# Key cache in 8 MB loads of 64 KB runs through three half-shared slots, value chunks in pairs behind them

## The chip, the cores and the metric

The kernel runs on one core of a Trainium2 chip. The metric is the device time of one execution in microseconds (us), taken as the median of several runs. The profile is one further execution, taken by the hardware profiler; its times count from the start of its span. TensorE is called PE there, VectorE DVE, ScalarE ACT, GpSimd POOL and SyncE SP.

## The reference

One decode step of a layer, for a batch of two, in float32:

```python
xn = layernorm(x)                                    # x: [2, 1, 512]
q = (xn @ wq) -> [2, 32 heads, 1, 128]
scores = q . k / sqrt(128)                           # k_cache: [2, 8, 32768, 128], 4 query heads share a key head
o = softmax(scores) . v                              # v_cache: the same shape
s = o -> [2, 1, 4096] @ wo
g = silu(relu(xn @ w1 + b1) ** 2 @ w2 + b2)
return x + s * g
```

Keys and values are 268.4 MB each, and each is read once; the weights are 24.1 MB together. The arithmetic on each byte is small.

## The kernel before, in words

A **stream** is one pair of batch and key head: there are 16 (`NS`), and a stream has 32768 keys and as many values of 128 numbers. A stream is cut into four **chunks** of 8192 keys, 4 MB each (`CHUNK`, 32 KB in each of the 128 partitions), so there are 64 chunks of keys and 64 of values (`NK`). Each is one DMA from SP's queue: `load_k` (L91) takes from each partition's 256 keys (128 KB in a row in memory) the quarter `u`, a run of 32 KB; `load_v` (L98) takes 4 MB in a row, 32 KB of it for each partition.

All big loads go through one ring of `BUFS` = 4 buffers of 32 KB (L55). The order of the loads is written out in the list `loads` (L126 to L136): the two halves of `wq`, then keys and values in turn, values four chunks behind the keys, `w1` and `w2` early on, `wo` last. A load is issued when `free` says that a buffer is there; `give()` frees one after the last instruction that reads it. So three loads are queued or on their way while one buffer is worked on.

The work on a chunk `n`:

- `scores(n)` (L237): eight DVE transposes (L246) of 128x1024 numbers turn the keys into `kt` tiles (a pool of 8 buffers); after each four of them PE multiplies the queries `qz` with them into the PSUM bank `sc[t]` (L251). Then `give()`, and a DVE maximum over the bank (`rm`, L255).
- `softmax(s)` (L257) after the fourth chunk: a short chain over DVE and PE finds the maximum (L259 to L268), four ACT exponentials (L272) fill `p`.
- `probs(s)` (L280): 16 PE transposes of `p` (L286) with four ACT copies to `pT` (L287), and a small product `l_ps` (L292) for the sum.
- `values(n)` (L302): 16 PE products of `pT` with the value chunk into `o_ps` (L309); the profile counts each as two instructions. After a stream's fourth chunk the result is scaled and turned into `oT` and `oW` (L316 to L329).

`mlp_up` and `mlp_down` (L334, L350) compute the gate early on. At the end `project` (L387) multiplies `oW` with `wo`, whose last quarter comes in four pieces, and L399 to L402 write the result.

The order of instructions on an engine isn't quite that of the text: the framework goes through the program with durations of its own, and an instruction whose inputs are there may be placed ahead of one that is written earlier and still waits. What each engine then executes is in that fixed order.

Of the kernel before, what the change touches and what calls it, by code (L numbers as in the profile page):

```python
# [9 lines left out]
F32 = mybir.dt.float32  # L10
# [4 lines left out]
P = 128  # L15
# [4 lines left out]

NG = 4
RUN = 64
CHUNK = P * RUN
NO = 16
BUFS = 4
NEG = -3.0e38
PIECES = ((0, 4), (4, 6), (6, 7), (7, 8))

# [2 lines left out]
def gqa_decode_kernel(ctx: ExitStack, tc: tile.TileContext, x, kc, vc, wq, wo, w1, b1, w2, b2, out):  # L33
    nc = tc.nc
    B, _, D = x.shape
# [4 lines left out]
    ND = D // P  # L40
# [11 lines left out]
    out2 = out.rearrange("b s d -> (b s) d")  # L52

    const = ctx.enter_context(tc.tile_pool(name="const", bufs=1))
    ring = ctx.enter_context(tc.tile_pool(name="ring", bufs=BUFS))  # L55
    ktpool = ctx.enter_context(tc.tile_pool(name="ktpool", bufs=8))
    work = ctx.enter_context(tc.tile_pool(name="work", bufs=2))
    pms = ctx.enter_context(tc.tile_pool(name="pms", bufs=2, space=bass.MemoryType.PSUM))
# [3 lines left out]
        return pms.tile([P, 512], F32, tag="ms", name=name)  # L62


    xt = const.tile([P, D], F32, name="xt")
    b1t = const.tile([NG, FG], F32, name="b1t")
    b2t = const.tile([1, D], F32, name="b2t")
    nc.vector.memset(xt, 0.0)
    nc.scalar.dma_start(xt[:B, :], x2)
    nc.scalar.dma_start(b1t, b1.rearrange("(g f) -> g f", g=NG))  # L70
# [8 lines left out]
    def rows(cache, s):  # L79
        hkv, b = divmod(s, B)  # L80
        return cache[b, hkv]

    def load_wq(i):
        t = ring.tile([P, 2, wq.shape[1]], F32, tag="r", name=f"wq{i}")
        nc.sync.dma_start(t, wq.rearrange("(p d) f -> p d f", p=P)[:, 2 * i:2 * i + 2, :])
        return t

    def load_k(m):
        s, u = divmod(m, NCH)
        t = ring.tile([P, RUN, DH], F32, tag="r", name=f"k{m}")  # L90
        nc.sync.dma_start(t, rows(kc, s).rearrange("(p t r) d -> p t r d", p=P, t=NCH)[:, u])  # L91
        return t

    def load_v(m):
        s, u = divmod(m, NCH)
        t = ring.tile([P, RUN, DH], F32, tag="r", name=f"v{m}")
        src = rows(vc, s)[u * CHUNK:(u + 1) * CHUNK].rearrange("(p r) d -> p r d", p=P)
        nc.sync.dma_start(t, src)  # L98
        return t

    def load_w1(_):
        t = ring.tile([P, ND, F], F32, tag="r", name="w1")
        nc.sync.dma_start(t, w1.rearrange("(p d) f -> p d f", p=P))
        return t

    def load_w2(_):
        t = ring.tile([P, FJ, D], F32, tag="r", name="w2")
        nc.sync.dma_start(t, w2.rearrange("(p j) e -> p j e", p=P))
        return t


    def load_wo(i):
        if i % 2 == 0:
            wide[i // 2] = ring.tile([P, 2, WG, D], F32, tag="r", name=f"wo{i // 2}")
        t = wide[i // 2][:, i % 2]
        src = wo[i * WG * P:(i + 1) * WG * P, :].rearrange("(p j) e -> p j e", p=P)
        if i < NWG - 1:
            nc.sync.dma_start(t, src)
        else:
            for j0, j1 in PIECES:  # L120
                nc.sync.dma_start(t[:, j0:j1, :], src[:, j0:j1, :])
        return t

    wide = {}
    NK = NS * NCH
    loads = [(1, load_wq, 0), (1, load_wq, 1)]  # L126
    for m in range(NK + NCH):
        if m < NK:
            loads.append((1, load_k, m))
        if m == 1:  # L130
            loads.append((1, load_w1, 0))
        if m == 2:
            loads.append((1, load_w2, 0))
        if m >= NCH:
            loads.append((1, load_v, m - NCH))
    loads += [(1 - i % 2, load_wo, i) for i in range(NWG)]  # L136
    free = [BUFS]
    done = [0]

    def issue():  # L140
        while done[0] < len(loads) and free[0] >= loads[done[0]][0]:
            bufs, f, a = loads[done[0]]
            free[0] -= bufs
            tiles[f, a] = f(a)
            done[0] += 1

    def take(f, a):
        return tiles.pop((f, a))

    def give():  # L150
        free[0] += 1
        issue()

    issue()
# [37 lines left out]
    nc.scalar.activation(st[:, 2:3], st[:, 1:2], AF.Sqrt)  # L192
    nc.vector.reciprocal(st[:, 3:4], st[:, 2:3])
    nc.vector.tensor_scalar(xn, xn, st[:, 3:4], None, op0=ALU.mult)  # L194
    xnT = const.tile([P, ND, P], F32, name="xnT")
# [3 lines left out]
    nc.vector.tensor_copy(xnT.rearrange("p a b -> p (a b)"), t_ps)  # L199


    for i in range(2):
        wqt = take(load_wq, i)
        for d2 in range(2):
            d = 2 * i + d2
            for f in range(2):
                for g in range(NG):
                    cc = f * NG + g
                    nc.tensor.matmul(sc[f][32 * g:32 * g + 32, :], xnT[:, d, 0:32],  # L209
                                     wqt[:, d2, cc * 512:(cc + 1) * 512], start=(d == 0), stop=(d == ND - 1))  # L210
        give()
    qT = const.tile([P, B, HKV, REP, 4], F32, name="qT")
    for f in range(2):
        for h in range(REP):
# [20 lines left out]
    rm, pr, pT, rs = {}, {}, {}, {}  # L235

    def scores(n):  # L237
        s, t = divmod(n, NCH)
        if t == 0:
            rm[s] = work.tile([P, NCH], F32, tag="rm4", name=f"rm4_{s}")  # L240
        kt = take(load_k, n)
        for e0 in range(0, 4, 2):
            kts = []
            for g in range(NG):
                r = ktpool.tile([P, 2, NO, 32], F32, tag="kt", name=f"kt{n}_{e0}_{g}")
                nc.vector.transpose(r.rearrange("p e o w -> p o e w"),  # L246
                                    kt[:, g * NO:(g + 1) * NO, e0 * 32:(e0 + 2) * 32].rearrange("p o (e w) -> p o e w", e=2))
                kts.append(r)
            for e in range(2):
                for g in range(NG):  # L250
                    nc.tensor.matmul(sc[t][32 * g:32 * g + 4 * REP, :], qz[s % 2][:, e0 + e, :],  # L251
                                     kts[g][:, e].rearrange("p o w -> p (o w)"),
                                     start=(e0 + e == 0), stop=(e0 + e == 3))
        give()
        nc.vector.tensor_reduce(rm[s][:, t:t + 1], sc[t], axis=AX.X, op=ALU.max)  # L255

    def softmax(s):  # L257
# [21 lines left out]

    def probs(s):  # L280
        p, lh = pr.pop(s)
        sb = work.tile([P, NG, 4, NO, REP], F32, tag="pT", name=f"pT{s}")
        for i in range(NO // 4):
            t_ps = misc(f"pT_ps{s}_{i}")
            for j in range(4):
                nc.tensor.transpose(t_ps[:, j * P:(j + 1) * P], p[:, 4 * i + j].rearrange("p w t -> p (w t)"), ident)  # L286
# [15 lines left out]
    def values(n):  # L302
# [3 lines left out]
        for i in range(NO // 4):  # L306
            for g in range(NG):
# [1 line left out]
                nc.tensor.matmul(o[32 * g:32 * g + 16, :], pT[s][:, g, a, 4 * i:4 * i + 4, :].rearrange("p o h -> p (o h)"),  # L309
                                 vt[:, lo:lo + 4, :].rearrange("p o d -> p (o d)"),  # L310
                                 start=(a == 0 and i == 0), stop=(a == NCH - 1 and i == NO // 4 - 1))
        give()
        if a == NCH - 1:
            hkv, b = divmod(s, B)
            o_sb = work.tile([P, 512], F32, tag="o_sb", bufs=1, name=f"o_sb{s}")
# [5 lines left out]
            nc.vector.tensor_copy(oT[:, hkv * REP:(hkv + 1) * REP, b], t_ps[:, :REP])  # L321
            if hkv % 2 == 1:
                i = hkv // 2
                m = work.tile([P, WG, P // WG], F32, tag="om", name=f"om{s}")
# [4 lines left out]
                nc.scalar.copy(oW[:, i, :, b], t_ps[:, :WG])  # L329


    hT, gate = const.tile([P, FJ, 32], F32, name="hT"), const.tile([P, DE], F32, name="gate")

    def mlp_up():  # L334
        wt = take(load_w1, 0)
# [6 lines left out]
        give()  # L342
# [7 lines left out]
    def mlp_down():  # L350
# [9 lines left out]
        give()  # L360
        e = work.tile([P, DE], F32, tag="e", name="e")
        nc.scalar.activation(e, y_ps[:, :DE], AF.Sigmoid)
        nc.vector.tensor_mul(gate, e, y_ps[:, :DE])


    for n in range(NK + NCH):
        s, t = divmod(n, NCH)
        if n < NK:
            if t == 0:
                set_q(s)  # L370
            scores(n)
        if n == 1:
            mlp_up()
        if n == 2:
            mlp_down()
        if s >= 1 and t == 0:
            probs(s - 1)
        if n < NK and t == NCH - 1:
            softmax(s)
        if n >= NCH:  # L380
            values(n - NCH)


    a_ps = sc[0]
# [9 lines left out]
        project(i, 0, WG)  # L394
    for j0, j1 in PIECES:
        project(NWG - 1, j0, j1)
    asb = work.tile([P, DE], F32, tag="e", name="a_sb")
# [28 lines left out]
```

## Time and profile before

| | |
|---|---|
| median of 3 runs | 1316.15 us (1316.07 to 1316.32) |
| profiled execution, its own time | 1315.98 us |
| its span, first to last instruction | 1314.2 us |
| bytes read from HBM | 561.01 MB, 427 GB/s over the span |
| PE busy / DVE busy / ACT busy | 946.4 us (72%) / 675.2 us (51%) / 107.5 us (8%) |
| mean granted TensorE clock | 0.861 |
| keys: DMAs, size, median from issue to landing | 64 of 4096 KB, 29.6 us |
| values: the same | 64 of 4096 KB, 29.6 us |

The profile's page lists busy times of the engines, a strip of 40 slices of the span with the busy share in tenths, the DMA queues, the chain of work that ended last, the costliest groups of instructions, and the DMA issues. Beside it the trace can be asked for the instructions in order of time (the timeline), for who waited for whom (the waits), for the chain in order of time, and for the busy time of each engine in chosen windows. It also holds a record of every DMA packet: its start, size and duration, and for each DMA the 16 completion marks of the 16 DMA engines. "Landing" is the moment at which the last of these is there.

### The profile page before, as it was taken

To read this page: it belongs to the slowest core of one execution; us is meant where nothing else is said; L and a number is where in the kernel's file an instruction comes from. 1 tells how busy PE (TensorE), PEld (TensorE's weight loads), DVE (VectorE), ACT (ScalarE), POOL (GpSimd) and SP (SyncE) were. 2 spreads that over 40 slices of the span, in tenths; PEclk is the share of its full clock that TensorE was granted. 3 is DMA by queue.
4 is the path that set the end of the run, shared out by engine and by line. 5 is a ranking of instruction groups with operands and counts; after the bars stand their busy time and mean duration, and the time that the engine had idled before them with its cause. 6 is when DMAs were issued, how large, how long until landed. Compare 5 with 4: busy or idle time off the path is not lost.

```text
span 1314.2 us, 11662 instructions
## 1 busy us (share of the span) xinstructions
PE 946.4 (72%) x5054; PEld 245.7 (19%) x5054; DVE 675.2 (51%) x778; ACT 107.5 (8%) x237; POOL 15.1 (1%) x76
## 2 busy tenths in 40 slices
PE   4777786876868677776776778586686767668666
PEld 1121121212112121111212112121211212112123
DVE  4765564553655465465454556355365546446510
ACT  0010000101001010100101001010100101010010
POOL 1000000000000000000000000000000000000000
PEclk9989888988888878887887988898887887888798
DMA  9999999999999999999999999999999999999997
GB/s 412 425 436 430 431 430 430 429 431 431 431 432 431 430 430 430 431 431 430 431 431 430 430 431 430 431 434 430 432 431 432 429 433 432 430 430 432 430 431 310
DMA packets 20113, 561.76 MB, mean 427 GB/s; under 512 B 2247, under 2 KB 2267, under 8 KB 2654
## 3 DMA queue, kind: packets, MB, share of 16 engines
q1 hardware_dynamic: 20024, 561.00, 99.3%
q8 instruction: 39, 0.64, 0.2%
q14 instruction: 12, 0.10, 0.0%
q10 hardware_dynamic: 38, 0.02, 0.0%
HBM read 561.01 MB, written 0.00 MB: 427 GB/s over the span
## 4 chain that ended last, share of the span: by engine, by line
DMA 76%; DVE 22%; PE 1%; issue 0%; ACTq 0%; DVEq 0%
DMA k<-in_A_k_cache 71%; DVE kt L246 22%; DMA v<-in_A_v_cache 2%; DMA wo<-in_A_wo 2%; PE sc L209 1%; DMA xt<-in_A_x 1%; PE y_ps L358 0%; PE sc L251 0%; PE xnT_ps L198 0%; DVE sq L189 0%; DVE xnT L199 0%; DVE st L190 0%; DVE st L186 0%; DVEq L246 0%; ACTq L70 0%
## 5 line engine op out<-in xcount | busy, mean ns | idle before, releaser
L251 PE MATMUL sc<-kt,qz 128*16 128x512 f32 x2048 | 605.6, 695 | 276.9 <-DVE kt L246 256.2
L246 DVE STREAM_TRANSPOSE kt<-k 128x1024 f32<-128x1024 f32 x512 | 584.3, 1207 | 288.3 <-DMA k<-in_A_k_cache 288.3
L309 PE MATMUL o_ps<-v,pT 128*16 128x512 f32 x2048 | 272.9, 604 | 11.5 <-DMA v<-in_A_v_cache 11.5
L251 PEld LDWEIGHTS sc<-kt,qz 128*16 128x16 f32 x2048 | 94.1, 100 | 768.9 <-DVE kt L246 652.0
L272 ACT ACTIVATE p<-sc,nm 128x512 f32<-128x512 f32 x64 | 68.8, 1198 | 1025.4 <-DVE nm L268 1025.4
L255 DVE TENSOR_REDUCE rm<-sc 128x1 f32<-128x512 f32 x64 | 44.3, 692 | 126.3 <-PE sc L251 126.3
L309 PEld LDWEIGHTS o_ps<-v,pT 128*16 128x16 f32 x2048 | 66.1, 98 | 169.9 <-issue 152.0
L286 PE MATMUL pT_ps<-ident,p 128*128 128x128 f32 x256 | 52.1, 381 | 0.1
L286 PEld LDWEIGHTS pT_ps<-ident,p 128*128 128x128 f32 x256 | 46.3, 205 | 5.6 <-issue 2.6
L320 PE MATMUL oT_ps<-rs,o_sb 128*128 128x4 f32 x128 | 19.2, 273 | 34.3 <-ACT o_sb L316 34.3
L275 DVE TENSOR_REDUCE l<-l 128x1 f32<-128x4 f32 x16 | 2.5, 154 | 66.9 <-ACT p L272 66.9
L294 DVE RECIPROCAL r<-l_ps 128x4 f32<-128x4 f32 x16 | 2.9, 183 | 56.5 <-PE l_ps L292 56.5
L321 DVE COPY oT<-oT_ps 128x4 f32<-128x4 f32 x16 | 2.6, 163 | 51.7 <-PE oT_ps L320 51.7
L287 ACT COPY pT<-pT_ps 128x256 f32<-128x256 f32 x64 | 23.9, 373 | 45.7 <-PE pT_ps L286 45.1
L320 PEld LDWEIGHTS oT_ps<-rs,o_sb 128*128 128x128 f32 x128 | 17.8, 215 | 48.3 <-ACT o_sb L316 48.3
L232 POOL COPY qz<-qT 32x16 f32<-32x16 f32 x64 | 12.8, 200 | 1081.4 <-PE sc L251 1051.2
L261 PE MATMUL mx_ps<-ident,rm 128*128 128x128 f32 x16 | 5.1, 319 | 15.8 <-DVE rm L259 15.8
L272 ACT ACTIVATION_READ_ACCUMULATOR p<-sc,nm 128x1 f32 x64 | 14.6, 228 | 0.0
L316 ACT COPY o_sb<-o_ps 128x512 f32<-128x512 f32 x16 | 9.7, 604 | 31.0 <-PE o_ps L309 31.0
L198 PE MATMUL xnT_ps<-ident,xn 128*128 128x128 f32 x4 | 1.1, 428 | 15.2 <-DVE xn L194 15.2
L390 PE MATMUL sc<-wo,oW 128*32 128x128 f32 x256 | 8.8, 275 | 3.4 <-DMA wo<-in_A_wo 3.3
L209 PE MATMUL sc<-wq,xnT 128*32 128x512 f32 x64 | 10.0, 792 | 0.8 <-DVE xnT L199 0.8
(67 smaller groups left out, 107.5 us busy)
## 6 DMA issues: line engine op xcount, KB each, us to landing
k<-in_A_k_cache SPq DMA_DIRECT2D x64, 4096.0 KB, 29.6
v<-in_A_v_cache SPq DMA_DIRECT2D x64, 4096.0 KB, 29.6
wq<-in_A_wq SPq DMA_DIRECT2D x2, 4096.0 KB, 12.2
w<-in_B_w SPq DMA_DIRECT2D x2, 3584.0 KB
wo<-in_A_wo SPq DMA_DIRECT2D x3, 2048.0 KB
wo<-in_A_wo SPq DMA_DIRECT2D x1, 1024.0 KB
wo<-in_A_wo SPq DMA_DIRECT2D x1, 512.0 KB
wo<-in_A_wo SPq DMA_DIRECT2D x2, 256.0 KB, 29.4
```

Source lines behind the costliest of these rows:

```text
L209: nc.tensor.matmul(sc[f][32 * g:32 * g + 32, :], xnT[:, d, 0:32], wqt[:, d2, cc * 512:(cc + 1) * 512], start=(d == 0), stop=(d == ND - 1))
L232: nc.gpsimd.tensor_copy(qz[s % 2][32 * a:32 * a + 32, :, a * REP:(a + 1) * REP], qT[32 * a:32 * a + 32, b, hkv].rearrange("p h e -> p e h"))
L246: nc.vector.transpose(r.rearrange("p e o w -> p o e w"), kt[:, g * NO:(g + 1) * NO, e0 * 32:(e0 + 2) * 32].rearrange("p o (e w) -> p o e w ...
L251: nc.tensor.matmul(sc[t][32 * g:32 * g + 4 * REP, :], qz[s % 2][:, e0 + e, :], kts[g][:, e].rearrange("p o w -> p (o w)"), start=(e0 + e = ...
L255: nc.vector.tensor_reduce(rm[s][:, t:t + 1], sc[t], axis=AX.X, op=ALU.max)
L272: nc.scalar.activation(p[:, :, :, t], sc[t].rearrange("p (o w) -> p o w", w=32), AF.Exp, bias=nm, scale=SCALE, accum_out=l4[:, t:t + 1])
L286: nc.tensor.transpose(t_ps[:, j * P:(j + 1) * P], p[:, 4 * i + j].rearrange("p w t -> p (w t)"), ident)
L287: nc.scalar.copy(sb[:, :, :, 4 * i:4 * i + 4, :].rearrange("p g a o h -> p o g a h"), t_ps.rearrange("p (o g y) -> p o g y", o=4, g=NG)[:, ...
L309: nc.tensor.matmul(o[32 * g:32 * g + 16, :], pT[s][:, g, a, 4 * i:4 * i + 4, :].rearrange("p o h -> p (o h)"), vt[:, lo:lo + 4, :].rearran ...
L316: nc.scalar.copy(o_sb, o)
L320: nc.tensor.matmul(t_ps[:, :REP], o_sb[:, i * DH:(i + 1) * DH], r4[:, i, :], start=(i == 0), stop=(i == 3))
L390: nc.tensor.matmul(a_ps[32 * g:32 * g + 32, :DE], oW[:, i, j, :], wot[i][:, j, g * DE:(g + 1) * DE], start=(i == 0 and j == 0), stop=(i == ...
```

## The change

- **Keys** come in 32 loads of 8 MB in place of 64 of 4 MB: `load_k(m)` takes half a stream, a run of 64 KB for each partition. They go to `kslots`, one tile of three slots of 32 KB: a stream's first load to slots 0 and 1, its second to slots 1 and 2. So that slot 1 is free early, the chunks of the first load are worked on in the order 1, 0 (`TS`, `key_slot`); those of the second in the order 2, 3. A key load is issued once the first chunk of the load before it has been worked on.
- **Values** have a pool of two buffers of 32 KB (`vpool`), with `wq`, `w1`, `w2` and half of `wo`. A value load is issued once `values` two chunks earlier is done. The last two value chunks and the other half of `wo` go to key slots.
- **Order of the loads**: a key load, then two value chunks, and so on. A stream's first two value chunks lie in the queue directly behind its last key load; the other two behind the first key load of the next stream.
- **Order of the work**: `softmax(s)`, `probs(s)` and `values` of the stream's first two chunks follow directly on its last `scores`; `values` of the other two follow on the next stream's first and second `scores`.
- **Space**: the big buffers grow from 128 KB to 160 KB of each partition. For that some small tiles share space (`first`, which the first `p` takes over) or have one buffer in place of two (`pT`, `om`, `e`), and a scratch area for DMA descriptors is set to 1024 bytes.

The diff, cut to what sets loads, order and waits:

```diff
-BUFS = 4
+TS = (1, 0, 2, 3)
...
-    ring = ctx.enter_context(tc.tile_pool(name="ring", bufs=BUFS))
+    vpool = ctx.enter_context(tc.tile_pool(name="vpool", bufs=2))
...
+    def key_slot(n):
+        return n // 2 % 2 + TS[n % NCH] % 2
+
     def load_k(m):
-        s, u = divmod(m, NCH)
-        t = ring.tile([P, RUN, DH], F32, tag="r", name=f"k{m}")
-        nc.sync.dma_start(t, rows(kc, s).rearrange("(p t r) d -> p t r d", p=P, t=NCH)[:, u])
-        return t
+        s, u = divmod(m, 2)
+        t = kslots[:, u:u + 2, :]
+        nc.sync.dma_start(t.rearrange("p i f -> p (i f)"),
+                          rows(kc, s).rearrange("(p u r) d -> p u (r d)", p=P, u=2)[:, u])
+        return None
...
+        if m < NK - 2:
+            t = vpool.tile([P, RUN, DH], F32, tag="v", name=f"v{m}")
+        else:
+            t = kslots[:, m - NK + 2].rearrange("p (r d) -> p r d", d=DH)
...
+    kslots = const.tile([P, 3, RUN * DH], F32, name="kslots")
+    loads = [(None, load_wq, 0), (None, load_wq, 1), (None, load_k, 0), (("q", 0), load_w1, 0), (("q", 1), load_w2, 0)]
+    for m in range(1, NK // 2):
+        loads.append((("s", 2 * m - 2), load_k, m))
+        for j in (2 * m - 2, 2 * m - 1):
+            loads.append((("w", j) if j < 2 else ("v", j - 2), load_v, j))
+    loads += [(("s", NK - 3), load_v, NK - 2), (("s", NK - 2), load_v, NK - 1)]
+    loads += [(("s", NK - 1), load_wo, 0), (("s", NK - 1), load_wo, 1), (("v", NK - 4), load_wo, 2), (("v", NK - 4), load_wo, 3)]
...
     def scores(n):
-        s, t = divmod(n, NCH)
-        if t == 0:
+        s, t = n // NCH, TS[n % NCH]
+        if n % NCH == 0:
...
-        kt = take(load_k, n)
+        if n % 2 == 0:
+            take(load_k, n // 2)
+        kt = kslots[:, key_slot(n)].rearrange("p (r d) -> p r d", d=DH)
...
-        give()
+        give("s", n)
...
-    for n in range(NK + NCH):
-        s, t = divmod(n, NCH)
-        if n < NK:
-            if t == 0:
-                set_q(s)
-            scores(n)
+    for n in range(NK):
+        s, i = divmod(n, NCH)
+        if i == 0:
+            set_q(s)
+        scores(n)
+        if i < 2 and s >= 1:
+            values(n - 2)
         if n == 1:
             mlp_up()
-        if n == 2:
             mlp_down()
-        if s >= 1 and t == 0:
-            probs(s - 1)
-        if n < NK and t == NCH - 1:
+        if i == NCH - 1:
             softmax(s)
-        if n >= NCH:
-            values(n - NCH)
+            probs(s)
+            values(n - 3)
+            values(n - 2)
+    values(NK - 2)
+    values(NK - 1)
```

More of the change, by code (lines that the diff above doesn't have):

```diff
@@ L62, in misc @@
         return pms.tile([P, 512], F32, tag="ms", name=name)
-    xt = const.tile([P, D], F32, name="xt")
+    first = work.tile([P, 4, D], F32, tag="p", bufs=1, name="first")
+    xt, b2t = first[:, 0], first[0:1, 1]
     b1t = const.tile([NG, FG], F32, name="b1t")
-    b2t = const.tile([1, D], F32, name="b2t")
     nc.vector.memset(xt, 0.0)
@@ L83, in load_wq @@
     def load_wq(i):
-        t = ring.tile([P, 2, wq.shape[1]], F32, tag="r", name=f"wq{i}")
+        t = vpool.tile([P, 2, wq.shape[1]], F32, tag="v", name=f"wq{i}")
         nc.sync.dma_start(t, wq.rearrange("(p d) f -> p d f", p=P)[:, 2 * i:2 * i + 2, :])
         return t
+    def key_slot(n):
+        return n // 2 % 2 + TS[n % NCH] % 2
     def load_k(m):
-        s, u = divmod(m, NCH)
-        t = ring.tile([P, RUN, DH], F32, tag="r", name=f"k{m}")
-        nc.sync.dma_start(t, rows(kc, s).rearrange("(p t r) d -> p t r d", p=P, t=NCH)[:, u])
-        return t
+        s, u = divmod(m, 2)
[3 more added lines that the diff above has]
+        return None
     def load_v(m):
         s, u = divmod(m, NCH)
-        t = ring.tile([P, RUN, DH], F32, tag="r", name=f"v{m}")
-        src = rows(vc, s)[u * CHUNK:(u + 1) * CHUNK].rearrange("(p r) d -> p r d", p=P)
-        nc.sync.dma_start(t, src)
+        if m < NK - 2:
+            t = vpool.tile([P, RUN, DH], F32, tag="v", name=f"v{m}")
+        else:
+            t = kslots[:, m - NK + 2].rearrange("p (r d) -> p r d", d=DH)
+        nc.sync.dma_start(t, rows(vc, s)[u * CHUNK:(u + 1) * CHUNK].rearrange("(p r) d -> p r d", p=P))
         return t
     def load_w1(_):
-        t = ring.tile([P, ND, F], F32, tag="r", name="w1")
+        t = vpool.tile([P, ND, F], F32, tag="v", name="w1")
         nc.sync.dma_start(t, w1.rearrange("(p d) f -> p d f", p=P))
@@ L106, in load_w2 @@
     def load_w2(_):
-        t = ring.tile([P, FJ, D], F32, tag="r", name="w2")
+        t = vpool.tile([P, FJ, D], F32, tag="v", name="w2")
         nc.sync.dma_start(t, w2.rearrange("(p j) e -> p j e", p=P))
@@ L113, in load_wo @@
         if i % 2 == 0:
-            wide[i // 2] = ring.tile([P, 2, WG, D], F32, tag="r", name=f"wo{i // 2}")
+            wide[i // 2] = (vpool.tile([P, 2, WG, D], F32, tag="v", name="wo") if i else
+                            kslots[:, 2].rearrange("p (i j e) -> p i j e", i=2, j=WG))
         t = wide[i // 2][:, i % 2]
@@ L125, in gqa_decode_kernel @@
     NK = NS * NCH
[L126 to L137, printed above, removed]
+    kslots = const.tile([P, 3, RUN * DH], F32, name="kslots")
[6 more added lines that the diff above has]
+    loads += [(("s", NK - 1), load_wo, 0), (("s", NK - 1), load_wo, 1), (("v", NK - 4), load_wo, 2), (("v", NK - 4), load_wo, 3)]
+    past = {None}
     done = [0]
     def issue():
-        while done[0] < len(loads) and free[0] >= loads[done[0]][0]:
-            bufs, f, a = loads[done[0]]
-            free[0] -= bufs
+        while done[0] < len(loads) and loads[done[0]][0] in past:
+            _, f, a = loads[done[0]]
             tiles[f, a] = f(a)
@@ L148, in take, with give @@
         return tiles.pop((f, a))
-    def give():
-        free[0] += 1
+    def give(*event):
+        past.add(event)
         issue()
@@ L194, in gqa_decode_kernel @@
     nc.vector.tensor_scalar(xn, xn, st[:, 3:4], None, op0=ALU.mult)
-    xnT = const.tile([P, ND, P], F32, name="xnT")
+    xnT = first[:, 2].rearrange("p (d b) -> p d b", d=ND)
     t_ps = misc("xnT_ps")
@@ L198, in gqa_decode_kernel @@
         nc.tensor.transpose(t_ps[:, d * P:(d + 1) * P], xn.rearrange("p (k d) -> p d k", d=ND)[:, d], ident)
-    nc.vector.tensor_copy(xnT.rearrange("p a b -> p (a b)"), t_ps)
+    nc.vector.tensor_copy(first[:, 2], t_ps)
     for i in range(2):
@@ L210, in gqa_decode_kernel @@
                                      wqt[:, d2, cc * 512:(cc + 1) * 512], start=(d == 0), stop=(d == ND - 1))
-        give()
+        give("q", i)
     qT = const.tile([P, B, HKV, REP, 4], F32, name="qT")
@@ L253, in scores @@
                                      start=(e0 + e == 0), stop=(e0 + e == 3))
-        give()
+        give("s", n)
         nc.vector.tensor_reduce(rm[s][:, t:t + 1], sc[t], axis=AX.X, op=ALU.max)
@@ L281, in probs @@
         p, lh = pr.pop(s)
-        sb = work.tile([P, NG, 4, NO, REP], F32, tag="pT", name=f"pT{s}")
+        sb = work.tile([P, NG, 4, NO, REP], F32, tag="pT", bufs=1, name=f"pT{s}")
         for i in range(NO // 4):
@@ L311, in values @@
                                  start=(a == 0 and i == 0), stop=(a == NCH - 1 and i == NO // 4 - 1))
-        give()
+        give("v", n)
         if a == NCH - 1:
@@ L323, in values @@
                 i = hkv // 2
-                m = work.tile([P, WG, P // WG], F32, tag="om", name=f"om{s}")
+                m = work.tile([P, WG, P // WG], F32, tag="om", bufs=1, name=f"om{s}")
                 nc.vector.tensor_mul(m, oT[:, i * WG:(i + 1) * WG, b:b + 1].to_broadcast([P, WG, P // WG]),
@@ L329, in values @@
                 nc.scalar.copy(oW[:, i, :, b], t_ps[:, :WG])
-    hT, gate = const.tile([P, FJ, 32], F32, name="hT"), const.tile([P, DE], F32, name="gate")
+    hT, gate = first[:, 3, :FJ * 32].rearrange("p (j b) -> p j b", j=FJ), const.tile([P, DE], F32, name="gate")
     def mlp_up():
@@ L341, in mlp_up @@
                                  start=False, stop=(d == ND - 1))
-        give()
+        give("w", 0)
         hr = work.tile([P, FG], F32, tag="tmp", name="hr")
@@ L359, in mlp_down @@
                                  start=False, stop=(j == FJ - 1))
-        give()
-        e = work.tile([P, DE], F32, tag="e", name="e")
+        give("w", 1)
+        e = work.tile([P, DE], F32, tag="e", bufs=1, name="e")
         nc.scalar.activation(e, y_ps[:, :DE], AF.Sigmoid)
         nc.vector.tensor_mul(gate, e, y_ps[:, :DE])
-    for n in range(NK + NCH):
-        s, t = divmod(n, NCH)
-        if n < NK:
-            if t == 0:
-                set_q(s)
-            scores(n)
+    for n in range(NK):
[5 more added lines that the diff above has]
+            values(n - 2)
         if n == 1:
             mlp_up()
-        if n == 2:
             mlp_down()
-        if s >= 1 and t == 0:
-            probs(s - 1)
-        if n < NK and t == NCH - 1:
+        if i == NCH - 1:
             softmax(s)
-        if n >= NCH:
-            values(n - NCH)
+            probs(s)
[3 more added lines that the diff above has]
+    values(NK - 1)
     a_ps = sc[0]
@@ L396, in gqa_decode_kernel @@
         project(NWG - 1, j0, j1)
-    asb = work.tile([P, DE], F32, tag="e", name="a_sb")
+    asb = work.tile([P, DE], F32, tag="e", bufs=1, name="a_sb")
     fin = const.tile([P, DE], F32, name="fin")
@@ L412 @@
     from concourse.bass_utils import run_bass_kernel_spmd
-    nc = bacc.Bacc("TRN2", target_bir_lowering=False, num_devices=1)
+    nc = bacc.Bacc("TRN2", target_bir_lowering=False, num_devices=1, dynamic_dma_scratch_size=1024)
     arrays, args = {}, {}
```

## The prediction, as put on record before the changed kernel ran

> **What bounds the kernel now.** I read the page's strip of 40 slices first.
>
> ```profile
> DMA  9999999999999999999999999999999999999997
> GB/s 412 425 436 430 431 430 430 429 431 431 431 432 431 430 430 430 431 431 430 431 431 430 430 431 430 431 434 430 432 431 432 429 433 432 430 430 432 430 431 310
> ```
>
> The DMA engines are full from the first slice to the last but one, at about 431 GB/s; PE (72%) and DVE (51%) are not. The chain of work says the same: keys landing and DVE transposes in turn, though a transpose only hands its buffer to a queue in which two more loads stand. From its rows at 587 to 666 us:
>
> ```profile
> 587.41 29.59 DMA k<-in_A_k_cache
> ...
> 617.10 9.14 DVE kt L246 x8
> ...
> 626.25 29.60 DMA k<-in_A_k_cache
> ...
> 655.95 9.14 DVE kt L246 x8
> ```
>
> From 617.10 to 655.95 four loads land (two of keys, two of values): 38.85 us, so 9.71 us for 4 MB. Only less transfer time, or an idle queue, can move the end.
>
> How full is full? The packet records give a duration by size: 8 KB 311 ns, 16 KB 613, 28 KB 1062, 32 KB 1215. From 16 to 32 KB that is 602 ns for 16 KB, so some 11 ns of a packet don't depend on its size. And the 16 DMA engines aren't abreast: the completion marks of one load lie 0.55 us apart at the start and 8.23 us near the end, since 39 packets of 16 KB that fetch instructions hit one engine each and set it back by some 1.4 us. The window from 1302 to 1309 us shows it: the DMA share is 0.56, most of the engines are done and the late ones set the end. With three loads queued the late engine never waits, and only its own delays count: 8.2 us over 16 streams, 0.5 us a stream.
>
> **The change, part by part.** Sums are made against the profiled execution (1315.98 us, span 1314.2), 0.17 us under the median of the runs shown.
>
> *Longer runs.* Each DMA engine moves 512 key packets of 32 KB now. If a run of 64 KB is one packet, 256 of the fixed parts go: 256 x 11 ns = 2.8 us; 32 fewer DMAs save a completion mark of 9 ns each on an engine, 0.3 us. All of it lies on the path: **-3.1 us**, 1312.9. Bounds: 0, if the run is cut into packets of 32 KB again, and -3.1 (the steps from 2 to 4 and from 8 to 16 KB give 9 ns, none gives more than 11). I take -3.1, from the step nearest in size. The Trainium skill ("DMA: Bandwidth & Descriptors", "Why a DMA increments its semaphore by 16 and not by 1") speaks of splitting for a row longer than 64 KiB; by it this run just fits one descriptor. No row here has such a packet.
>
> *Work that only moves.* The number of transposes, products, exponentials and bytes stays. `first`, single `pT`, `om` and `e` add waits for readers that ended a stream earlier or, for `first`, with `mlp_down` (75.97 us in the timeline, and `p` is first written after that): 0, hidden by the transfers. The tail keeps its 8 MB of `wo` behind the last values: 0.
>
> *The new waits.* SP's queue is in order, so a load that waits holds all behind it. Let L be the start of the transposes when a stream's last key load (chunks 4s+2, 4s+3) lands. Behind it stand two value chunks and the next key load, 4 x 9.71 = 38.8 us of transfers. The key load needs the first chunk's transposes, L+9.1, against L+19.4 where the queue reaches it: slack. The next value loads, 4s, 4s+1 of the stream, wait for `values` of the last stream's end: done long before. But the load behind the next keys, v(4s+2), needs the buffer of v(4s), so it needs the end of `values(4s)`, behind both chunks, `softmax` and `probs`. That is the new chain, 15 times (the last stream's values go to key slots). Its rows, from the last stream, where the same steps follow each other:
>
> ```profile
> 1241.78 9.13 DVE L246 STREAM_TRANSPOSE kt<-k 128x1024 f32<-128x1024 f32 x8 [7.62 <-DMA k<-in_A_k_cache]
> ...
> 1252.89 0.69 DVE L255 TENSOR_REDUCE rm<-sc 128x1 f32<-128x512 f32 x1 [1.98 <-PE sc L251]
> 1253.62 0.16 DVE L259 TENSOR_REDUCE rm<-rm 128x1 f32<-128x4 f32 x1
> ...
> 1259.25 0.24 ACT L272 ACTIVATION_READ_ACCUMULATOR p<-sc,nm 128x1 f32 x1
> ...
> 1261.91 3.61 PE L286 MATMUL pT_ps<-ident,p 128*128 128x128 f32 x16
> ...
> ```
>
> ```profile
> 1280.58 6.23 PE L309 MATMUL o_ps<-v,pT 128*16 128x512 f32 x32 [6.09 <-DMA v<-in_A_v_cache]
> ```
>
> - Both chunks. As written, transposes, 1.98 us for PE's last products, 0.69 for the maximum, twice: 11.80 + 11.70 = 23.5 us (start of one chunk 1241.78 to end of its maximum 1253.58; 44.21 to 55.91 for two in a row at the start). But both chunks land together, so the second one's transposes are ready while the first maximum waits, and the framework places ready work ahead: at 93.05 us four transposes of the next stream stand inside the first softmax. Then it is 18.2 + 0.7 + 2.0 + 0.7 = **21.6 us**. I take this.
> - Maximum to last exponential: 1253.58 to 1259.49, 5.9 us; 0.1 to PE.
> - PE's transposes to the start of `values`: 1261.91 to 1265.57, 3.7 us.
> - `values`: 3.63 us with PE at full clock (1265.57), 6.23 after 6.1 us of idleness (granted clock 0.59 there). PE now idles some 6.7 us ahead of `probs`; the low clock lasts 3.4 or 6.8 us at a time in the clock's records, and the transposes use up 3.7 of it (their row already had 0.72). I add 0.6, bounds 0 and 1.4. The Trainium skill ("TensorE: Matmul & The Clock Gate", "Part 1: The HAM clock gate") gives about 3.4 us of work to get back to full clock; by that I would add 0, but the records here go to 6.8.
>
> Sum: 21.6 + 5.9 + 0.1 + 3.7 + 3.6 + 0.6 = L + 35.5 us for the issue (34.9 to 36.3).
>
> The deadline: the key load ahead has its last packet at L + 38.8 - 0.6 (last mark to first transpose, 0.55) = L + 38.2. A DMA's first packet starts 1.0 us after issue (wq: 0.74 to 1.755), and 12.2 us to landing for wq, less 9.7 and 0.55, gives 1.9 with the slow first packets of an empty queue. So the issue must come by L + 36.3 to 37.2, and it comes at 35.5: **0.8 to 1.7 us to spare**, none in the worst corner. The queue just doesn't run dry for the late engine. The early ones do wait, and can lead by no more than this spare time; a fetch on one of them costs the rest of its 1.4 us. I take **+0.3 us** in all, bounds 0 and 5 (0.3 us a stream).
>
> Forecast: 1315.98 - 3.1 + 0.3 = 1313.2, read as **1313 us**, with 1311.5 (one fetch of 1.4 us fewer on the late engine) to 1314.5 as its own range.
>
> **The rivals.**
>
> *The deadline is missed (slower).* One mechanism: if the framework leaves the maximum of the first chunk ahead of the second chunk's transposes, the chain is 23.5 + 13.9 = L + 37.4 and the issue is 0.2 to 1.1 us late. It decides from L + 36.3 (or 37.2). Each stream then loses that, 15 x 0.7 = 10 us, and all DMA engines start abreast each time, so that fetches on different engines add up: 0.5 us a stream becomes some 1.2, 10 us more. 1312.9 + 20 = 1333, from 1319 (0.4 us a stream) to 1343. For it: within a chunk's wait no row of the profile shows a following transpose, as no two chunks landed together. Against it: the row at 93.05, and products of L390 that stand among L320's at 1298.54.
>
> *The run is cut again, or the spare time eats the gain.* Packets of 32 KB as before, or a residue of 2 to 5 us: 1315.98 + 0.3 = 1316, from 1314.5 to 1319. For it: no packet over 32 KB in the trace. Against it: sizes of 2 to 32 KB all go as whole runs.
>
> *The waits are coarser.* If a read of one key slot waited for the load into the others, `scores` of a second chunk would wait for the next key load, some 30 us a stream, 15 x 30 = 450: about 1765. Against it: the pieces of one `wo` tile are waited for one by one (L390 at 1304.97, 1307.53, 1309.99). Any other wait of a few us a stream falls between this and the first rival.
>
> **How the numbers follow.** Forecast 0.42, most of it (0.34) beyond 0.2% below the median (under 1313.5), about what a measurement of this kernel can tell from no change; the second rival 0.20, nearly all within; the missed deadline 0.30; coarser or longer waits, over 1343, 0.05; under 1311.5, 0.03. So faster 0.37, same 0.26, slower 0.37. The range 1311.5 to 1335 leaves out 0.03 below, 0.05, and some 0.07 of the first rival.
>
> **What would show it.** Packets of 64 KB near 2.42 us. In DVE's order, transposes of the second chunk ahead of the first maximum. SP's wait for L309 before every fourth value load, ending some 35.5 us after the transposes of a stream's last keys began, and a first packet that follows the last one without a gap. A gap there of over 0.5 us, or DMA slices under 430 GB/s throughout, would make the forecast wrong; so would marks of one load that still spread by 8 us late in the run, since the queue would then be deeper than I reckon.

## The result, and the profile after

The changed kernel takes **1324.15 us** (median of 6 runs, 1320.82 to 1326.11), the kernel before 1316.28 beside it (6 runs): ratio **1.0057**, interval 1.0046 to 1.0068. It is slower by 7.9 us, where 1313 was forecast. The forecast's sign was wrong; the time lies inside its range, among the times of the first rival (1319 to 1343). The runs of the changed kernel lie 5.3 us apart, those of the kernel before 1.4. The profiled execution is the slowest of the six: 1326.11 us, span 1324.3.

The strip of 40 slices of the changed kernel, its main queue (packets, MB, share of 16 engines) and its chain of work by engine:

```profile
DMA  9999999999999999999999999999999999999997
GB/s 412 440 429 403 430 430 435 440 411 426 406 440 442 410 434 409 429 425 434 438 419 439 415 430 426 443 432 398 433 426 436 437 420 430 416 435 420 435 430 325
...
DMA packets 15505, 561.75 MB, mean 424 GB/s; under 512 B 1735, under 2 KB 1755, under 8 KB 2142
...
q1 hardware_dynamic: 15416, 561.00, 98.9%
...
DMA 75%; DVE 19%; issue 4%; PE 1%; ACT 0%; SPq 0%; DVEq 0%; ACTq 0%
```

The row of nines hides the loss. The row of GB/s shows it: before, nearly every slice stood at 429 to 434; now slices at 398 to 420 stand between slices at 425 to 443. Something holds up part of the DMA engines once a stream (some 78.7 us, 2.4 slices), and afterwards they run as before.

The waits of SP's queue (what it waited for: us in total, times, longest) point to the wait for the buffer of `values`. Before the change it was:

```profile
SPq L98 <- PE o_ps L309: 315.2, 60, 7.0
```

After it, with the wait for a key slot below:

```profile
SPq L106 <- PE o_ps L316: 569.0, 60, 26.0
SPq L96 <- DVE kt L253: 280.4, 31, 9.2
```

Of the 60, the one before v(4s+2), behind a stream's two chunks, `softmax` and `probs`, is the new chain. The timeline of the changed kernel for one such stream (start, duration, engine, line; in brackets the idle time before and who ended it):

```profile
631.93 11.38 DVE L253 STREAM_TRANSPOSE kt<-kslots 128x1024 f32<-128x1024 f32 x10 [12.73 <-DMA kslots<-in_A_k_cache]
...
643.24 0.65 DVE L262 TENSOR_REDUCE rm<-sc 128x1 f32<-128x512 f32 x1
...
643.82 6.85 DVE L253 STREAM_TRANSPOSE kt<-kslots 128x1024 f32<-128x1024 f32 x6
...
652.65 0.69 DVE L262 TENSOR_REDUCE rm<-sc 128x1 f32<-128x512 f32 x1 [1.98 <-PE sc L258]
...
658.87 0.23 ACT L279 ACTIVATION_READ_ACCUMULATOR p<-sc,nm 128x1 f32 x1
...
659.15 3.68 PE L293 MATMUL pT_ps<-ident,p 128*128 128x128 f32 x16 [5.24 <-ACT p L279]
...
662.98 7.63 PE L316 MATMUL o_ps<-v,pT 128*16 128x512 f32 x64
...
667.25 3.76 SPq L106 DMA_DIRECT2D v<-in_A_v_cache  x2
```

Ten transposes stand ahead of the first maximum: two of the second chunk fill the wait, as assumed. From the first transpose to the issue it is 667.25 - 631.93 = 35.3 us, against 35.5 forecast; over the 15 streams it is 34.6 to 35.7. So the chain was sized well, and the load that waits for it still comes too late for most of the DMA engines. The windows of the changed kernel at a later stream (issue at 903.92) show that; the last two columns are the share of the 16 DMA engines and GB/s:

```profile
900.00:903.00 3.00, 3.00 (x31) 1.05 (x34) 0.36 (x2) 0.37 (x1) 0.00 (x0) 1.00 0.86 371
903.00:906.00 3.00, 3.00 (x33) 0.82 (x28) 0.00 (x0) 0.00 (x0) 0.00 (x0) 1.00 0.71 213
906.00:909.00 3.00, 1.30 (x14) 0.12 (x4) 0.96 (x1) 0.00 (x0) 0.00 (x0) 1.00 0.82 350
```

The same three windows of the kernel before, where the queue stays full:

```profile
900.00:903.00 3.00, 3.00 (x32) 0.85 (x28) 0.69 (x1) 0.00 (x0) 0.00 (x0) 1.00 0.99 426
903.00:906.00 3.00, 2.11 (x14) 0.31 (x6) 0.00 (x0) 0.00 (x0) 0.00 (x0) 1.00 1.04 448
906.00:909.00 3.00, 0.00 (x0) 0.00 (x0) 0.00 (x0) 0.00 (x0) 0.00 (x0) 1.00 0.94 404
```

Single windows wobble, since they are hardly longer than a packet of 64 KB; over the three it is 311 GB/s after and 426 before. The packet records tell which engines lose (they don't name the engine; I string them together, each packet behind the one that ended last before it). The key load ahead ends at 903.37 us on the earliest DMA engine and at 907.54 on the latest, 4.2 us apart. The value load's first packets can start 0.95 us after the issue, at 904.9. Engines that were done by then have stood idle, and start again with packets of 32 KB that take 1.6 to 2.2 us; the latest engine was still busy at 904.9 and goes on with one of 1.22. Of the 15 x 16 first packets of these loads in the run, **180 of 240 take over 1.3 us** (median of all 240 is 1.73), where 1.215 is the usual duration. I call such a place a *choke* below, and such an engine *restarted*, though not every one of them has stood idle, as the text under the table of steps shows.

That gives a budget, the mean over the 16 DMA engines, from the packet records:

| | before | after |
|---|---|---|
| busy with data, us | 1304.4 | 1309.0 |
| of it, slow packets of 32 KB (time over 1.215) | 2.1 | 10.5 |
| idle between first and last 20 us | 0.0 | 5.9 |
| idle at the end (late engines alone) | 3.3 | 2.1 |
| end of the data | 1309.5 | 1319.3 |

Slow packets rise by 8.4 and all other data work falls by 3.8. The longer runs alone, forecast as 3.1, don't give that much: with the chain cut short (below) the same sum falls by 1.8. The other 2.0 us are packets that are shorter here than there, slow ones left out (64 KB 2422.9 ns on average against 2426.3, 32 KB 1214.5 against 1216.5); why is not shown. Then 5.9 us of idle time come in and 1.2 at the end go: 8.4 - 3.8 + 5.9 - 1.2 = 9.3 of the 9.8 us between the two ends.

### The profile page after: what moved, and what is told of

Read it like the earlier page. It is cut to its first block, busy times and chain, and to the rows that moved or that the text cites. A ratio compares the mean times of both kernels' runs of the same rounds, so it can differ in the third digit from the quotient of the medians.

```text
span 1324.3 us, 11665 instructions
## 1 busy us (share of the span) xinstructions
PE 880.5 (66%) x5054; PEld 246.3 (19%) x5054; DVE 669.9 (51%) x778; ACT 107.8 (8%) x237; POOL 14.9 (1%) x76
## 4 chain that ended last, share of the span: by engine, by line
DMA 75%; DVE 19%; issue 4%; PE 1%; ACT 0%; SPq 0%; DVEq 0%; ACTq 0%
DMA kslots<-in_A_k_cache 73%; DVE kt L253 19%; DMA wo<-in_A_wo 2%; DMA wq<-in_A_wq 1%; PE o_ps L316 0%; ACT p L279 0%; PE pT_ps L293 0%; PE sc L398 0%; PE sc L258 0%; DVE rm L262 0%; PE mx_ps L268 0%; SPq L127 0%; DVE mh L270 0%; DVE a_sb L407 0%; DVE fin L408 0%
## 5 line engine op out<-in xcount | busy, mean ns | idle before, releaser
L253 DVE STREAM_TRANSPOSE kt<-kslots 128x1024 f32<-128x1024 f32 x512 | 583.7, 1207 | 329.6 <-DMA kslots<-in_A_k_cache 329.6
L258 PE MATMUL sc<-kt,qz 128*16 128x512 f32 x2048 | 548.1, 635 | 298.2 <-DVE kt L253 276.5
L316 PE MATMUL o_ps<-v,pT 128*16 128x512 f32 x1984 | 245.5, 607 | 3.1 <-DMA v<-in_A_v_cache 3.1
L258 PEld LDWEIGHTS sc<-kt,qz 128*16 128x16 f32 x2048 | 89.4, 97 | 727.4 <-DVE kt L253 593.9
L293 PE MATMUL pT_ps<-ident,p 128*128 128x128 f32 x256 | 58.0, 421 | 83.8 <-ACT p L279 83.8
L316 PEld LDWEIGHTS o_ps<-v,pT 128*16 128x16 f32 x1984 | 60.2, 98 | 154.0 <-issue 138.0
L293 PEld LDWEIGHTS pT_ps<-ident,p 128*128 128x128 f32 x256 | 51.0, 221 | 87.9 <-ACT p L279 86.8
L279 ACT ACTIVATION_READ_ACCUMULATOR p<-sc,nm 128x1 f32 x64 | 13.9, 218 | 0.0
L214 PE MATMUL sc<-wq,first 128*32 128x512 f32 x64 | 9.8, 778 | 0.8 <-DVE first L204 0.8
L221 DVE COPY qr<-sc 128x512 f32<-128x512 f32 x8 | 5.3, 684 | 9.6 <-PE sc L214 9.0
```

What stands on the lines that cost most here:

```text
L221: nc.vector.tensor_copy(qr, sc[f][:, h * DH:(h + 1) * DH].rearrange("p (e w) -> p e w", e=4)[:, :, None, :] .to_broadcast([P, 4, 4, 32]))
L253: nc.vector.transpose(r.rearrange("p e o w -> p o e w"), kt[:, g * NO:(g + 1) * NO, e0 * 32:(e0 + 2) * 32].rearrange("p o (e w) -> p o e w ...
L279: nc.scalar.activation(p[:, :, :, t], sc[t].rearrange("p (o w) -> p o w", w=32), AF.Exp, bias=nm, scale=SCALE, accum_out=l4[:, t:t + 1])
```

## The experiments

Two theories could explain a loss at the choke of this kind. **Restart**: the load comes in time for the late DMA engine and too late for the early ones, which run dry, wait, and start again slowly. **Transfer**: the loss has nothing to do with the chain; the long packets or the order of the loads make transfers slower. A third, the prediction's first rival, says that the whole queue runs dry (**hard deadline**): the loss then vanishes all at once when the chain is shorter than the deadline. Each experiment is timed beside the kernel before (1316.2 to 1316.3).

**The chain cut short.** The first two value chunks of each stream from the second on are multiplied before `softmax`, by the probabilities of the stream before (this changes the output). The load behind the next keys then waits for much less; transfers, packets and sizes are those of the changed kernel.

```
     if i == NCH - 1:
+        if s:
+            values(n - 3)
+            values(n - 2)
         softmax(s)
         probs(s)
-        values(n - 3)
-        values(n - 2)
+        if not s:
+            values(n - 3)
+            values(n - 2)
...
+    w = pT[s - 1] if s and a < 2 else pT[s]
```

> The values of a stream's first two chunks are taken ahead of its softmax, weighted with the probabilities of the stream before (so that half of each stream's sum is weighted with another stream's numbers); all loads, products and bytes stay. The value load behind the next keys can then be issued some 11 us earlier. Restart theory (the loss is paid at that load, since early DMA engines run out of work there and start again with slow packets): 1312 to 1314.5 us, no packets over 1.3 us at that load, marks of one load spread by 6 us and more late in the run. Transfer theory (loads of 8 MB in packets of 64 KB, or values in pairs, move slower by themselves): stays at 1320 to 1326.

Measured: **1315.28 us** (1314.36 to 1315.58), ratio 0.9990 [0.9981, 0.9999], some 0.8 us over the expected range. The strip, and the issue in the same stretch:

```profile
GB/s 416 438 424 412 432 431 443 439 420 429 433 433 440 430 428 435 428 433 431 441 426 434 427 431 432 436 433 440 423 428 431 440 430 436 425 428 430 430 435 305
```

```profile
646.99 13.91 SPq L106 DMA_DIRECT2D v<-in_A_v_cache  x2
```

The load is issued 19.6 us after the transposes began (627.38) and not 35.3 us after. Of the first packets, 14 of 240 are slow, all in the first stream, which was left as it was; idle time 0.4 us, slow packets 2.0. The dips below 420 are gone, but for the fourth slice (412), which holds the first stream. The same 64 KB packets in the same order cost nothing: the transfer theory falls. The gain over the kernel before is 1.0 us, though, and not 3.1; see below.

**The chain by steps.** One exponential of each `softmax` is 1.0 us of the chain. From the second stream on one or three of the four are left out (the output is another), or the first one, or all four, are run again. The diff shows the forms for one; for three it is `NCH - 3`, for four `range(4)`.

```
-        for t in range(NCH):
+        for t in range(NCH - 1 if s else NCH):
             nc.scalar.activation(p[:, :, :, t], ...)
...
+        for t in range(1):
+            nc.scalar.activation(p[:, :, :, t], ...)
```

> From the second stream on, one of the four exponentials is left out (the first stream's numbers stand in its place, so the output is another one): the chain from a stream's last keys to its first values is 1.0 us shorter, all loads stay. Restart theory: what matters is not whether the latest DMA engine runs dry but how many of the earlier ones do; their marks spread by 2 to 4 us, so 1 us more to spare saves a part only: 1317 to 1321 us. Rival, a hard deadline that the kernel misses by some tenths of a us in each stream: all of the loss goes at once, 1313 to 1315.

> As the run with one exponential left out, but with three left out: the chain is 3.1 us shorter. Restart theory: some 5 us to spare, so nearly no engine runs dry any more: 1314.5 to 1317 us. Rival, a hard deadline: 1313 to 1315, the same as with one left out.

> The first exponential of each softmax is done once more (the same numbers): the chain is 1.0 us longer. With 4.0 us more a stream took 81.94 us, so the chain alone sets 77.94 + 1.0 = 78.94 us a stream here; with delays that don't make up for each other some 79.3 to 79.7 in place of 78.73. Restart theory: 1324 + 15 x 0.6 to 1.0 = 1332 to 1339 us. Rival, a hard deadline already missed: the full 1.0 us a stream, 1339.

> The four exponentials of each softmax are done twice (the same numbers once more), 4.0 us longer on the chain from a stream's last keys to its first values. Restart theory: now the latest DMA engine runs dry too, by 4.0 less the some 2.3 us that it had to spare, 15 times, and all start again slowly: 1324 + 25 to 45 = 1350 to 1370 us. Transfer theory: the chain isn't what costs the time, 1322 to 1330.

Measured, in the order of the chain's length. "Issue" is the time from the first transpose of the last keys to the issue of the value load, the median of the streams from the second on (single streams lie within 1.2 us of it); "restarted" the slow first packets, over 1.3 us, of 240; idle and slow packets are means of the 16 engines:

| | issue, us | restarted | idle, us | slow packets, us | time, us | ratio to before |
|---|---|---|---|---|---|---|
| chain cut short | 19.6 | 14 | 0.4 | 2.0 | 1315.28 | 0.9990 [0.9981, 0.9999] |
| three exponentials less | 31.6 | 48 | 1.2 | 3.6 | 1315.52 | 0.9993 [0.9984, 1.0003] |
| one less | 34.4 | 137 | 2.2 | 7.6 | 1321.28 | 1.0035 [1.0022, 1.0048] |
| the change | 35.2 | 180 | 5.9 | 10.5 | 1324.15 | 1.0057 [1.0046, 1.0068] |
| one more | 36.0 | 223 | 14.0 | 11.2 | 1331.98 | 1.0118 [1.0101, 1.0135] |
| four more | 39.4 | 233 | 55.0 | 11.0 | 1372.94 | 1.0427 [1.0411, 1.0443] |

With one exponential less the hard deadline asked for 1313 to 1315; it is 1321.28, and that rival falls. The loss fades over some 4 us of the chain, and the restarted engines fade with it.

What decides is when an engine ends the key load, counted from the issue of the value load. In the changed kernel, of the engines that ended it less than 0.95 us after the issue, and so had to wait, 80 of 80 begin with a slow packet. Of those that ended it 0.95 to 1.7 us after the issue, which waited little or not at all, it is still 72 of 77; from 1.7 to 2.5 us 19 of 42, and later 9 of 41. At the issue at 667.25 shown above, 11 of 16 first packets are slow, though the 16 engines together stood idle for some 0.5 us only. With one exponential less, only 19 of the 137 slow packets belong to engines that ended before 0.95 us. So the restart theory has the right place and the right cause, a late issue, but too narrow a condition: an engine loses without having run dry, if the load comes less than some 1.7 us before its last packet ends.

At the long end the picture is the rival's: 1.0 us more of chain adds 7.8 us in 15 chokes, half of it each time; with 4.0 us more it is 48.8 us, 3.3 each time, and all 16 engines end the key load before the next can start. Here the windows of the longest chain (same columns as above), around its issue at 693.00:

```profile
690.00:693.00 3.00, 3.00 (x32) 0.75 (x28) 0.62 (x1) 0.00 (x0) 0.00 (x0) 1.00 0.03 5
693.00:696.00 3.00, 3.00 (x32) 0.81 (x27) 3.00 (x4) 0.00 (x0) 0.00 (x0) 1.00 0.79 251
696.00:699.00 3.00, 3.00 (x22) 0.56 (x16) 3.00 (x3) 0.00 (x0) 0.00 (x0) 1.00 1.04 448
```

A DMA share of 0.03 is a queue that has run dry; the window after it, at 251 GB/s, holds the wait for the first packets and the slow restart of all engines. That one came out at 1372.94, a little over its expected 1350 to 1370; one less (1321.28) and one more (1331.98) lie just outside theirs, three less within. Note also that slow packets stop growing (10.5, 11.2, 11.0) once nearly every engine restarts, while idle time goes on: two separate terms, both from the same late issue.

**The last keys of a stream in two loads.** The other way to gain time for the chain: the first half of a stream's last keys lands earlier, so that its transposes are done when the second half lands.

```
+        if u == 0:
             nc.sync.dma_start(t.rearrange("p i f -> p (i f)"), ...)
+        else:
+            for h in range(2):
+                nc.sync.dma_start(t[:, h], rows(kc, s).rearrange("(p t r) d -> p t (r d)", p=P, t=NCH)[:, 2 + h])
```

> Only a stream's second key load is split into two of 4 MB with runs of 32 KB, the one that is worked on first ahead, so the chain from its landing starts some 9.7 us earlier; nothing else changes. Restart theory: no engine runs dry, half of the gain in packets stays: 1316.2 - 1.5 = 1314 to 1316 us. Transfer theory: half of the large packets and all pairs of values are still there: 1318 to 1322.

Measured: **1315.13 us** (1314.91 to 1316.94, 11 runs), ratio 0.9994 [0.9985, 1.0003]; idle 0.0, slow packets 1.8 us. The strip has no dips:

```profile
GB/s 416 428 430 431 432 431 432 436 424 432 432 431 438 427 437 425 432 431 432 438 424 436 429 431 431 433 439 425 434 429 432 438 426 436 426 431 432 432 431 309
```

By its median it is the fastest kernel of the study, 1.2 us under the kernel before, but its interval touches 1. Half of the key packets are still of 64 KB, so half of the gain was to be had, 1.5 us by the prediction's 3.1.

**All keys in loads of 4 MB.** Every key load is cut in two at the same place, so that no packet is over 32 KB while the order and the chain stay: in the last load of a stream the half that is used first is issued last.

```
+        for h in ((0, 1), (1, 0))[u]:
+            nc.sync.dma_start(t[:, h], rows(kc, s).rearrange("(p t r) d -> p t (r d)", p=P, t=NCH)[:, 2 * u + h])
```

> Every key load is split into two of 4 MB with runs of 32 KB, issued back to back with the one that is worked on first behind the other, so that the chain starts when it did; order, waits and bytes stay as in the changed kernel. Restart theory: the same loss, without the gain of the longer packets: 1325 to 1330 us. Transfer theory with the 64 KB packets as the culprit: 1314 to 1318; with the pairs of values as the culprit: as the restart theory.

Measured: **1325.20 us** (1323.87 to 1326.12), ratio 1.0067 [1.0054, 1.0081]. The slowness stays without any long packet, so the packets don't cause it. It is 1.05 us slower than the changed kernel, less than its runs lie apart, with somewhat cheaper chokes (idle 4.0 and slow packets 8.7 us against 5.9 and 10.5). Packets and loads were cut together, so neither has a price of its own here. The Trainium skill ("SBUF — State Buffer", "The DMA setup-cost knee") gives every transfer some 2 us that don't depend on its size, and advises the largest single transfer. By that, 32 loads fewer would save an estimated 64 us; the measurement decides, and it says 1.05 us for shorter packets and more loads together, or some 5 us if the cheaper chokes are set against it (1.05 + 1.9 + 1.8), for loads that stand behind others in a queue. The same section's limit of 436 GB/s lies just over the 429 to 434 of most slices before the change; single slices of the changed kernel, up to 443, are above it.

**Instruction fetches.** The prediction held packets that fetch instructions responsible for the spread of the engines in the kernel before (0.55 us at the start, 8.23 near the end). This is the kernel before, with 120 tiny fills on GpSimd more per chunk of keys, to add instructions to fetch.

```
+                if e0 == 0 and g == 0:
+                    nc.gpsimd.tensor_copy(dummy, r[0:1, 0, 0, 0:8])
+                    for _ in range(120):
+                        nc.gpsimd.memset(dummy, 0.0)
```

> The kernel before with 120 tiny fills more on GpSimd for each chunk of keys (7680 in all, into 32 bytes that nothing reads). If packets that fetch instructions are what sets single DMA engines back, some 30 more of them over some 10 engines, 1.4 us each, make the latest engine some 4 us later: 1318.5 to 1322 us, with more packets in the instruction queue and marks that spread by some 12 us late in the run. If the spread has another cause: 1316 to 1317.

Measured: **1350.73 us** (1350.40 to 1351.18), ratio 1.0262 [1.0246, 1.0277]: far over the expectation. GpSimd's packets of instructions rose from 12 to 73:

```profile
q14 instruction: 73, 0.60, 0.1%
```

All of these hit one DMA engine: the interval between its completion marks of successive loads is 0.64 us longer with one such packet in it (median of 61 intervals) than with none (58), and on the first engine there is no difference. Its marks fall behind the first engine's by 2.9, 5.5, 8.1, 10.8, 13.4, 16.1 and 19.0 us in successive streams, and stay between 13.9 and 19.1 from there on; it ends its data 17 us after the others. So fetches do set single engines back, one packet of 8 KB by 0.64 us. But the fills themselves are 28% of this kernel's chain of work, DVE waited 190.8 us in sum for GpSimd, and the other 15 engines end some 18 us later than before, so the 34 us of time aren't the price of the fetches alone, and that share is not settled here.

## Why the prediction was wrong, point by point

- *DMA bounds the kernel.* Right: the chain of work is still 75% DMA and 19% transposes, and each time above, but that with more instruction fetches, goes with the DMA engines' idle time and packets.
- *A run of 64 KB is one packet, -3.1 us.* Right in its mechanism: 4096 packets of 65,536 B, 2418 ns each where 2.42 us was forecast. But the size was wrong by more than half: with the chain cut short the gain is 1.0 us. The fixed part of a packet is not 11 ns. The records of two packets that follow each other on an engine overlap by 3 to 4 ns, whatever their size; from start to start it is 1215.3 ns for 32 KB before and 2423.0 ns for 64 KB here, so a packet saved is worth 7.6 ns, 256 of them 1.9 us. Against that, the 528 value and other packets of 32 KB on an engine follow each other 1.4 ns later than before, 0.7 us, and 0.4 us are idle time. That leaves 0.8 us, close to the 1.0 measured.
- *The new chain, 35.5 us.* Right: 35.3 in the stream shown (34.6 to 35.7 in the run), the second chunk's transposes ahead of the first maximum as assumed. From the start of `values` to the issue it is 4.3 us (662.98 to 667.25), so the 3.6 + 0.6 for it held, though the clock's records of the kernel before have stretches at the low clock of 10.2 and 13.7 us too, and not of 3.4 and 6.8 alone.
- *The deadline of the late engine, 0.8 to 1.7 us to spare.* Right, and on the safe side: the latest engine had 1.65 to 3.2 us left at every choke, counted from the issue plus 0.95 us. It never ran dry; nor did it with one exponential more (0.6 to 1.9 us left), which took 1331.98 us.
- *"The early ones do wait, and can lead by no more than this spare time; a fetch on one of them costs the rest of its 1.4 us. I take +0.3 us in all, bounds 0 and 5."* **This step failed.** It measured about 11 us in the forecast's own sum (1324.15 - 1312.9), and 8.9 us against the same kernel with the chain cut short (1324.15 - 1315.28). The engines that wait don't just lose a lead they had no use for. Their first packets take some 1.9 us and not 1.215, and most of those that end less than 1.7 us after the issue, without a wait, take 1.5 to 1.9: 8 to 16 engines at each choke are slow. By the end that is 8.4 us of slow packets on each engine, with 5.9 us of idle time on top. The engines are also kept close to the latest one, 1.9 to 4.2 us apart at the chokes, so the early ones gather no lead that would cover their delays. The prediction had the slow first packets of an empty queue in hand and used them only for the deadline of the late engine, the one engine that didn't run dry.
- *The first rival, 1333.* It had the right place and the right sign, but not the right condition: its point of decision, L + 36.3 us, was for the latest engine. The loss starts some 4 us earlier, with the earliest. One exponential more takes the chain to 36.0 us (35.5 to 36.7), about the rival's point, and that kernel's 1331.98 lies near the rival's 1333; but its latest engine still had time to spare, so the agreement is luck.
- *The signs to look for.* A gap, slices under 430 GB/s: the GB/s row showed it. Marks spread by 8 us, as a sign of a deeper queue, are seen where the queue is deep: 8.3 with the last keys in two loads and 8.9 with the chain cut short, against 1.9 to 4.2 at the chokes of the changed kernel.

What stays open: why an engine that doesn't wait starts a late load slowly too, why in some chokes the three or four packets after the first take 1.3 to 1.6 us too, and how much of the slowness is the empty queue itself, how much that many engines start at one time.

## What to carry to other kernels

Where transfers bound a kernel, count the spare time of a load against the *earliest* DMA engine, not against the landing of the load ahead: the engines were 2 to 4 us apart here, up to 9 where the queue is deep. Leave some 2 us more: engines that ended less than 1.7 us after the issue paid too. A load that waits until the last one in the queue is nearly through costs waiting and slow packets, even if the slowest engine never notices; the DMA row of the strip stays full of nines, so read its GB/s and the first packets behind the wait. Larger loads make the chain to the next issue longer, because they land later as a whole; cut the one load at the head of that chain, and leave the others whole. Here that took back the loss, to 1315.13 us, and showed no clear gain over the kernel before.

## What the hardware showed beside this

- A DMA engine that has run dry starts again with a packet of 32 KB of 1.89 us (median of 240 in the longest chain, where all had run dry), up to 2.5, where one in a full queue takes 1.215. One that ends its last load less than 1.7 us after the next was issued starts about as slowly, without a wait (72 of 77).
- The first packet starts 0.96 to 0.98 us after an issue into a queue that is dry (all 15 issues of the longest chain; 0.95 at 667.25 in the changed kernel). The Trainium skill ("DMA: Bandwidth & Descriptors", "Latency and other measured facts") gives about 600 ns for the first byte; the measured 0.95 is longer, and the one used here.
- The lead of the early engines over a late one is bounded here: with one engine set back by fetches the marks of a load spread to 19.1 us, just under two loads of 4 MB (2 x 9.71), and no further.
- GpSimd's instruction packets, 73 of 8 KB, all hit the same DMA engine and set it back by 0.64 us each.
